# A fused attention and two-layer feed-forward kernel: third tile's loads tied behind the weight loads, VectorE's second conversion pass into a free slot

## Chip, cores and metric

One NeuronCore of a Trainium2 chip runs the whole program in one launch. The metric is the device time of one execution, in microseconds: the median of three runs. TensorE (PE in the profile) multiplies, VectorE (DVE), ScalarE (ACT) and GpSimd (POOL) work elementwise, SyncE (SP) issues most of the transfers.

## What is computed

The weights w_in, w_out (and those of the second layer) come as 64-bit floats, so the kernel converts them itself.

```python
B, H, S, D = 4, 8, 576, 64
# windowed attention: each query sees itself and the 63 keys before it
scores = q @ k.T / sqrt(D); mask = (rel >= 0) & (rel < 64)
attn_out = softmax(scores, mask) @ v            # (4, 8, 576, 64)
x = attn_out.transpose(0, 2, 1, 3).reshape(2304, 512)
# first layer: w_in 512 x 2048, w_out 2048 x 512
h = x @ w_in
g = where(h >= 1, h, where(h <= -1, 0, (h + 1)**2 / 4))
y = g @ w_out
# second layer: w_in 512 x 1024, w_out 1024 x 512, gain g_ln
h = y @ w_in2; s = h * softmax(h)
out = (((s - mean(s)) / sqrt(var(s) + 1e-6)) * g_ln) @ w_out2
```

## The kernel before

Attention works on 12 tiles of 192 tokens, and in each on 4 pairs of heads; g counts these groups (tile t = g // 4). For a group `st_qkt` transposes Q and K into the buffers kq (for the first three tiles on TensorE, L334, with copies by VectorE and ScalarE; from the fourth tile on by VectorE's transposes, L325 and L326), `st_s` makes scores and exponentials, `st_norm` divides, `st_t` transposes the probabilities and `st_v` multiplies by V and leaves x as a high and a low part (xh, xl).

The first layer goes over 6 blocks j of 384 tokens (two tiles) and in each over 16 slices f of 128 columns. `moe_h` makes h of a slice (12 matmuls, L496: high times high, high times low, low times high), `moe_g` and `moe_g2` make g (ScalarE L505, L506 and L512, VectorE's u pass L511), `moe_g3` its low part gl (L516; GpSimd in block 0), `moe_y` adds the slice into four accumulators (L527). Block 0 is special in that the weights arrive while it runs, and in that its two tiles are taken one after the other for the first two slices.

The weights of the first layer are 32 units of 512 KB, two per slice: for slice f the unit of w_in (number 2f + 1) and that of w_out (2f + 2). A unit goes through these steps:

1. load into one of NST = 5 staging buffers `wst` (`w_unit`, L124 and L126, on the SP queue). A staged value is a pair of 32-bit words, low and high;
2. `split_a`: ScalarE rescales the high word (L132);
3. `split_b`: VectorE shifts the low word (L136), then joins the two words (L137). Before, L137 writes its result back over the high word, so with a step of two words;
4. `split_c`: ScalarE casts the result to the high half wih or woh (L145), GpSimd subtracts it for the low half wil or wol (L146). Before, both read the staging buffer, so it is free for the next load when L146 is done.

`w_conv` takes each unit in flight one step on, and is called once per group in the opening and twice per slice after it. Each of the 64 halves has a slot of its own, [128, 512] of 32 bits, in the pool w_p (tags wih0 to wih15, wil, woh, wol); the slots of wih12 to wih15 and wil12 to wil15 hold Q and K of the first two tiles at first. The third tile's Q and K (`qkn`, `load_qk(2 * NP)`) and later ones (`qk`) have five buffers of their own, V (`vw`) has six.

The order on each engine's queue is made by a scheduler: it takes the instructions that the program's text lists, and moves those ahead whose inputs it reckons to be ready. `tc.issue_after(x)` keeps what is issued under it behind the instruction x. `after(fn, a)` uses it for loads: before, x is the first weight load, `wdma[0]`, so that the scheduler was free to put them almost anywhere. On its queue each engine takes its instructions strictly in that order, SP its transfers too.

Of the kernel before, what the change touches and what calls it, by code (L numbers as in the profile page):

```python
# [8 lines left out]
F32 = mybir.dt.float32  # L9
F32R = mybir.dt.float32r  # L10
U32 = mybir.dt.uint32
# [9 lines left out]
def kernel(  # L21
# [12 lines left out]
    nc = tc.nc  # L34
# [83 lines left out]

    wdma = []

    def w_unit(src, hi, lo, gain=None, eng=nc.sync):
        st = stage["p"].tile([128, 512, 2], U32, tag="st", bufs=NST, name="wst")
        if src.shape[0] == 128 and len(src.shape) == 3:
            w_dma = eng.dma_start(out=st.rearrange("p (k f) t -> p k (f t)", k=src.shape[1]), in_=src)  # L124
        else:
            w_dma = eng.dma_start(out=st.rearrange("p f t -> p (f t)"), in_=src)  # L126
        wdma.append(w_dma.ins)
        return st, hi, lo, gain

    def split_a(st, *_):  # L130
        val = st[:, :, 1].bitcast(F32)
        nc.scalar.activation(val, val, ACTF.Prelu, scale=2.0 ** -112, alpha=2.0 ** 32)  # L132

    def split_b(st, *_):
        low, high = st[:, :, 0], st[:, :, 1]
        nc.vector.tensor_scalar(low, low, 29, None, op0=ALU.logical_shift_right)  # L136
        nc.vector.scalar_tensor_tensor(  # L137
            high, high, 3, low, op0=ALU.logical_shift_left, op1=ALU.bitwise_or
        )

    def split_c(st, hi, lo, gain):
        val = st[:, :, 1].bitcast(F32)
        if gain is not None:
            nc.scalar.activation(val, val, ACTF.Copy, scale=gain)
        nc.scalar.copy(hi, val)  # L145
        nc.gpsimd.tensor_tensor(lo, val, as_f32(hi), op=ALU.subtract)  # L146
# [16 lines left out]
        return w_p.tile([128, 512], F32R, tag=tag, name=tag)  # L163

    def w1_unit(f, which):
        if which == 0:
            hi, lo = wtile(f"wih{f}"), wtile(f"wil{f}")
            wih[f] = hi.rearrange("p (k f) -> p k f", k=KC)
            wil[f] = lo.rearrange("p (k f) -> p k f", k=KC)
            src = w_in[:, f * 256:(f + 1) * 256].rearrange("(k p) f -> p k f", p=128)  # L170
        else:
            hi, lo = woh[f], wol[f] = wtile(f"woh{f}"), wtile(f"wol{f}")
            src = w_out[f * 128:(f + 1) * 128, :]
        return w_unit(src, hi, lo)

# [18 lines left out]
    def w2_step(n, act, dve):  # L196
        for age, do in ((0, None), (4, split_a), (5, split_b), (6, split_c)):
# [6 lines left out]
            with tc.issue_after(act), tc.issue_after(dve):  # L204
                if age < 6:
                    do(*w2_units[u])
                    continue
                st, _, _, gain = w2_units.pop(u)
                if u < 8:
                    z = stage["p"].tile([128, 512], F32, tag="st", bufs=NST, name="w2st")  # L210
                    nc.scalar.copy(z, st[:, :, 1].bitcast(F32))
                    nc.gpsimd.dma_start(out=w2d[u], in_=z)
                    continue
                z = stage["p"].tile([128, 2, 512], F32R, tag="st", bufs=NST, name="w2st")
                do(st, z[:, 0, :], z[:, 1, :], gain)
                nc.gpsimd.dma_start(out=w2d[u], in_=as_f32(z.rearrange("p t f -> p (t f)")))

    def w2_load(n):
# [325 lines left out]


    def after(fn, a):
        with tc.issue_after(wdma[0]):
            fn(a)

    def w_load(n=1):  # L550
# [13 lines left out]
    for n in range(G0 + 4):  # L564
# [3 lines left out]
            st_norm(n - 1)  # L568
        if 0 <= n - 2 <= G0:
            st_t(n - 2)  # L570
        if n == NQ:
            after(load_qk, 2 * NP)
        if n == NV:
            after(load_v, 2)
        if n + 2 <= G0 + 1:
            st_qkt(n + 2)
        if 0 <= n - 3 < G0:
# [23 lines left out]
    def slots():  # L601
        for g in range(G0 + 1, GB + 1):
            st_s(g)
            yield
            st_v(g - 1)
            st_norm(g)
            yield
            qkt_and_loads(g + 1)
            v_ahead(g)
            yield  # L610
            st_t(g)
            if g == GB:
                st_s(g + 1)
            yield
# [370 lines left out]
```

## Time and profile before

| what | before |
|---|---|
| three runs, us | 709.12, 710.65, 710.14 (median 710.14) |
| profiled execution, us | 712.67 |
| its span | 710.9 |
| TensorE busy, share of span | 96% |
| VectorE, ScalarE, GpSimd busy | 61%, 58%, 27% |
| DMA moved | 88.94 MB, mean 125 GB/s |
| mean granted TensorE clock (share of full) | 0.993 |

The span runs from the first to the last instruction of the program; the execution has 1.8 us around it. Shares are averages over stages with different limits: the opening with the conversion of the weights (to some 123 us), the rest of the first layer (to some 520 us), the second layer.

### The profile page before, as it was taken

The numbers are of one execution on the slowest core, as the hardware profiler recorded it, in microseconds if no ns is written. First come the engines' busy times: TensorE is split into PE (matmuls) and PEld (weight loads), VectorE is DVE, ScalarE is ACT, GpSimd is POOL, SyncE is SP. The second block draws the span as 40 slices with busy tenths as digits, with TensorE's granted clock in tenths as the row PEclk, the third lists the DMA queues.
The fourth block names the chain that finished last, engine by engine and source line by source line (L and its number), as shares of the span: only waits on it lengthen the run. The fifth ranks groups of instructions, "written<-read, shape, count | busy, mean of one in ns | idle before, by whom it ended". The sixth has DMA issues, their size and how long they took to land.

```text
span 710.9 us, 12663 instructions
## 1 busy us (share of the span) xinstructions
PE 685.6 (96%) x4439; PEld 630.0 (89%) x4439; DVE 434.3 (61%) x1147; ACT 413.0 (58%) x1006; POOL 195.3 (27%) x217
## 2 busy tenths in 40 slices
PE   6899978999999999999999999999999899999998
PEld 5689768999999999999999999999988678888887
DVE  4549898555555555454455543642379799988850
ACT  5778886565566655565566665454455635545541
POOL 2358876200001000021112111652472223300000
PEclk9989999999999999999999999999999999999999
DMA  9986897534353623346352211452033554553321
GB/s 193 216 231 171 220 260 189 107 81 107 71 110 88 139 61 73 78 124 130 87 112 70 95 60 47 154 200 89 1 126 97 175 164 155 175 177 122 131 74 45
DMA packets 155544, 88.94 MB, mean 125 GB/s; under 512 B 118616, under 2 KB 141400, under 8 KB 155480
## 3 DMA queue, kind: packets, MB, share of 16 engines
q1 hardware_dynamic: 144040, 64.00, 36.4%
q0 software_dynamic: 8704, 19.41, 8.4%
q10 hardware_dynamic: 2736, 4.72, 1.8%
q8 instruction: 35, 0.57, 0.4%
q14 instruction: 29, 0.24, 0.1%
HBM read 63.97 MB, written 24.12 MB: 124 GB/s over the span
## 4 chain that ended last, share of the span: by engine, by line
PE 72%; DVE 10%; issue 7%; POOL 4%; DMA 3%; ACT 2%; SPq 1%; DVEq 0%; POOLq 0%; ACTq 0%
PE ps_h L496 22%; PE acc L527 22%; PE ps_o L826 13%; PE P L711 7%; PE ps_x L476 2%; PE ps_p L402 2%; PE ps_s L442 2%; PE ps_s L352 2%; DVE wst L137 2%; POOL wil L249 2%; DVE wst L136 1%; PE ps_x L421 1%; DMA wst<-in_moe_w_out_dram 1%; DVE gl L516 1%; DVE s L740 1%
## 5 line engine op out<-in xcount | busy, mean ns | idle before, releaser
L511 DVE SCALAR_TENSOR_TENSOR u<-u,ps_h 128x384 f32<-128x384 f32 (+1 forms) x98 | 53.2, 543 | 143.8 <-ACT u L506 140.2
L496 PE MATMUL ps_h<-xh,wih 128*128 128x384 f32 (+1 forms) x392 | 132.6, 339 | 3.2 <-DVE u L511 3.1
L496 PE MATMUL ps_h<-xl,wih 128*128 128x384 f32 (+1 forms) x392 | 131.5, 336 | 1.4 <-DVE xl L429 1.4
L527 PE MATMUL acc<-gl,woh 128*128 128x384 f32 (+1 forms) x392 | 130.7, 335 | 2.2 <-DVE gl L516 1.3
L496 PE MATMUL ps_h<-xh,wil 128*128 128x384 f32 (+1 forms) x392 | 131.5, 336 | 0.0
L527 PE MATMUL acc<-gh,wol 128*128 128x384 f32 (+1 forms) x392 | 129.7, 333 | 0.0
L527 PE MATMUL acc<-gh,woh 128*128 128x384 f32 (+1 forms) x392 | 126.9, 342 | 0.0
L505 ACT ACTIVATE u<-ps_h,half 128x384 f32<-128x384 f32 (+1 forms) x98 | 55.9, 572 | 92.6 <-PE ps_h L496 92.4
L512 ACT CAST gh<-u 128x384 fp32r<-128x384 f32 (+1 forms) x98 | 49.7, 507 | 55.0 <-DVE u L511 37.8
L496 PEld LDWEIGHTS ps_h<-xh,wih 128*128 128x128 f32 x392 | 74.6, 190 | 5.2 <-DVE u L511 4.7
L527 PEld LDWEIGHTS acc<-gl,woh 128*128 128x128 f32 x392 | 73.8, 188 | 3.5 <-DVE gl L516 1.7
L496 PEld LDWEIGHTS ps_h<-xl,wih 128*128 128x128 f32 x392 | 74.7, 190 | 2.2 <-DVE xl L429 2.0
L516 DVE TENSOR_TENSOR gl<-u,gh 128x384 fp32r<-128x384 f32 x80 | 52.8, 661 | 37.3 <-ACT gh L512 36.7
L527 PEld LDWEIGHTS acc<-gh,woh 128*128 128x128 f32 x392 | 72.4, 188 | 3.0 <-issue 2.4
L496 PEld LDWEIGHTS ps_h<-xh,wil 128*128 128x128 f32 x392 | 74.7, 190 | 0.1
L527 PEld LDWEIGHTS acc<-gh,wol 128*128 128x128 f32 x392 | 73.7, 188 | 0.0
L711 PE MATMUL P<-wih,x2p 128*128 128x512 f32 x216 | 70.6, 391 | 0.5 <-DVE xo L539 0.5
L826 PE MATMUL ps_o<-woh,wol 128*128 128x512 f32 (+1 forms) x152 | 58.6, 385 | 2.9 <-DVE wol L814 2.9
L826 PE MATMUL ps_o<-woh,woh 128*128 128x512 f32 (+1 forms) x152 | 58.4, 384 | 0.0
L826 PE MATMUL ps_o<-wol,woh 128*128 128x512 f32 (+1 forms) x152 | 58.0, 382 | 0.0
L506 ACT ACTIVATE u<-u 128x384 f32<-128x384 f32 (+1 forms) x98 | 51.0, 521 | 2.0
L711 PEld LDWEIGHTS P<-wih,x2p 128*128 128x128 f32 x216 | 40.5, 188 | 9.2 <-DVE xo L539 0.9
(125 smaller groups left out, 1250.8 us busy)
## 6 DMA issues: line engine op xcount, KB each, us to landing
vw<-in_v_dram SPq DMA_DIRECT2D x32, 256.0 KB, 5.2
wst<-in_moe_w_in_dram SPq DMA_DIRECT2D x16, 512.0 KB, 5.2
wst<-in_moe_w_out_dram SPq DMA_DIRECT2D x16, 512.0 KB, 5.5
lnd<-e SPq DMA_DIRECT2D x16, 512.0 KB, 2.7
lT<-lnd SPq DMA_DIRECT2D x64, 128.0 KB, 3.0
x2d<-xo POOLq DMA_DIRECT2D x24, 192.0 KB, 2.5
out_dram<-o ACTq DMA_DIRECT2D x17, 256.0 KB, 2.9
wst<-in_moe_w_in_dram POOLq DMA_DIRECT2D x8, 512.0 KB, 5.3
```

Source lines behind the costliest of these rows:

```text
L137: nc.vector.scalar_tensor_tensor(high, high, 3, low, op0=ALU.logical_shift_left, op1=ALU.bitwise_or)
L249: nc.gpsimd.tensor_tensor(lo, v_, as_f32(hi), op=ALU.subtract)
L352: nc.tensor.matmul(ps[:, i * 128 + c0:i * 128 + 128], qT[g][:, i, :, :].rearrange("p x q -> p (x q)"), kT[g][:, i * 64 + c0:i * 64 + 128], ...
L496: nc.tensor.matmul(ps, a, bb[:, kc, c], start=(n == 0), stop=(n == 3 * KC - 1))
L505: nc.scalar.activation(u, ps, ACTF.Relu, bias=half, scale=0.5)
L506: nc.scalar.activation(u, u, ACTF.Square)
L511: g = nc.vector.scalar_tensor_tensor(u, u, 1.0, ps, op0=ALU.min, op1=ALU.max)
L512: return nc.scalar.copy(hi, u).ins, g.ins
L516: eng.tensor_tensor(lo, u, as_f32(hi), op=ALU.subtract)
L527: nc.tensor.matmul(acc[j, e][:, c], a, bb, start=(f == 0 and n == 0 and c.start == 0), stop=(f == NF - 1 and n == 2),)
L711: nc.tensor.matmul(ps, l, r, start=(n == 0), stop=(n == 5))
L826: nc.tensor.matmul(ps, a[kk // 4][:, kk % 4, :], b[kk][:, c:c + w], start=(n == 0), stop=(n == 3 * NK2 - 1),)
```

## The change

Two edits. First, `split_b` gets a target `val`: for a w_in unit of slice f that is the slot of woh f, for a w_out unit of slice f the slot of wih f + 3, as long as that exists (f + 3 < 16); both slots are still empty then. The last three w_out units and the units of the second layer keep the high word in the staging buffer as their target. L137 (L139 in the changed kernel) writes there with a step of one word, and `split_c` reads there. Second, `after` ties to the newest weight load instead of the first, the third tile's Q and K are issued three rounds later in the opening (`n == G0 + 3`), and its V when the slots begin.

```diff
-    def w_unit(src, hi, lo, gain=None, eng=nc.sync):
+    def w_unit(src, hi, lo, gain=None, eng=nc.sync, val=None):
...
-        return st, hi, lo, gain
+        if val is None:
+            val = st[:, :, 1].bitcast(F32)
+        return st, val, hi, lo, gain
...
-    def split_b(st, *_):
+    def split_b(st, val, *_):
         low, high = st[:, :, 0], st[:, :, 1]
         nc.vector.tensor_scalar(low, low, 29, None, op0=ALU.logical_shift_right)
         nc.vector.scalar_tensor_tensor(
-            high, high, 3, low, op0=ALU.logical_shift_left, op1=ALU.bitwise_or
+            val.bitcast(U32), high, 3, low, op0=ALU.logical_shift_left, op1=ALU.bitwise_or
         )
 
-    def split_c(st, hi, lo, gain):
-        val = st[:, :, 1].bitcast(F32)
+    def split_c(_, val, hi, lo, gain):
...
     def w1_unit(f, which):
+        tag = f"wih{f + 3}" if which else f"woh{f}"
+        val = w_p.tile([128, 512], F32, tag=tag, name="wv") if f + 3 * which < NF else None
...
-        return w_unit(src, hi, lo)
+        return w_unit(src, hi, lo, val=val)
...
     def after(fn, a):
-        with tc.issue_after(wdma[0]):
+        with tc.issue_after(wdma[-1]):
             fn(a)
...
-        if n == NQ:
+        if n == G0 + 3:
             after(load_qk, 2 * NP)
-        if n == NV:
-            after(load_v, 2)
...
             st_norm(g)
+            if g == G0 + 1:
+                after(load_v, 2)
```

In the rows of order below, a name's number tells one buffer from another. The SP queue in the opening, from the third unit on, before (L279 is Q and K of the third tile, L291 of the fourth, L302 V of the third):

```order
L124 DMA wst_170<-in_moe_w_in_dram 128x4x256
L126 DMA wst_174<-in_moe_w_out_dram 128x1024
L124 DMA wst_178<-in_moe_w_in_dram 128x4x256
L279 DMA qkn_438<-in_q_dram 96x8x64
L279 DMA qkn_439<-in_q_dram 96x8x64
L279 DMA qkn_440<-in_k_dram 128x8x64
L279 DMA qkn_441<-in_k_dram 128x8x64
L291 DMA qk_964<-in_q_dram 32x6x32 x4
L291 DMA qk_964<-in_k_dram 32x6x32 x4
L126 DMA wst_365<-in_moe_w_out_dram 128x1024
L124 DMA wst_413<-in_moe_w_in_dram 128x4x256
L302 DMA vw_474<-in_v_dram 128x8x64
```

And in the changed kernel (three lines further on):

```order
L124 DMA wst_173<-in_moe_w_in_dram 128x4x256
L126 DMA wst_178<-in_moe_w_out_dram 128x1024
L124 DMA wst_183<-in_moe_w_in_dram 128x4x256
L126 DMA wst_371<-in_moe_w_out_dram 128x1024
L124 DMA wst_420<-in_moe_w_in_dram 128x4x256
L126 DMA wst_462<-in_moe_w_out_dram 128x1024
L124 DMA wst_491<-in_moe_w_in_dram 128x4x256
L126 DMA wst_516<-in_moe_w_out_dram 128x1024
L282 DMA qkn_518<-in_q_dram 96x8x64
L282 DMA qkn_519<-in_q_dram 96x8x64
L282 DMA qkn_520<-in_k_dram 128x8x64
L282 DMA qkn_521<-in_k_dram 128x8x64
```

Five units, 6 to 10, have moved ahead of the third tile's Q and K; the fourth tile's loads, not seen here, now come after unit 21.

VectorE between the conversion of the third unit and the second u pass, before (rows of scores and softmax left out at the "..."):

```order
L137 SCALAR_TENSOR_TENSOR wst_170<-wst_170 128x512
L136 TENSOR_SCALAR wst_178<-wst_178 128x512
...
L137 SCALAR_TENSOR_TENSOR wst_174<-wst_174 128x512
L137 SCALAR_TENSOR_TENSOR wst_178<-wst_178 128x512
...
L511 SCALAR_TENSOR_TENSOR u_562<-u_562,ps_h_549 128x192
...
L337 COPY kq0_124<-ps_t_600 64x3x64
L429 TENSOR_TENSOR xl_310<-ps_x_580,xh_309 128x192
L511 SCALAR_TENSOR_TENSOR u_640<-u_640,ps_h_627 128x192
```

And in the changed kernel:

```order
L139 SCALAR_TENSOR_TENSOR wv_170<-wst_173 128x512
...
L139 SCALAR_TENSOR_TENSOR wv_175<-wst_178 128x512
...
L139 SCALAR_TENSOR_TENSOR wv_180<-wst_183 128x512
...
L139 SCALAR_TENSOR_TENSOR wv_368<-wst_371 128x512
L514 SCALAR_TENSOR_TENSOR u_567<-u_567,ps_h_554 128x192
...
L139 SCALAR_TENSOR_TENSOR wv_417<-wst_420 128x512
...
L139 SCALAR_TENSOR_TENSOR wv_459<-wst_462 128x512
...
L139 SCALAR_TENSOR_TENSOR wv_488<-wst_491 128x512
L139 SCALAR_TENSOR_TENSOR wv_513<-wst_516 128x512
L514 SCALAR_TENSOR_TENSOR u_653<-u_653,ps_h_640 128x192
```

The second conversion passes of units 6 to 10 now stand ahead of the second u pass, and the copy of the third tile's Q (kq0) behind it.

ScalarE around that copy, in the changed kernel (L146 is the cast to the high half, L134 `split_a`, L410 a copy of transposed probabilities, L509 the square and L515 the cast of g, L341 and L342 the copies of Q and K of the third tile's first group):

```order
L146 CAST wih3_418<-wv_417 128x512
L146 CAST woh2_369<-wv_368 128x512
L134 ACTIVATE wst_516<-wst_516 128x512
L509 ACTIVATE u_653<-u_653 128x192
L146 CAST wih4_489<-wv_488 128x512
L410 COPY pT_620<-ps_p_619 128x384
L146 CAST woh3_460<-wv_459 128x512
L515 CAST gh_654<-u_653 128x192
L146 CAST woh4_514<-wv_513 128x512
L341 COPY kq0_124<-ps_t_611 64x3x64
L342 COPY kq0_124<-ps_t_611 128x256
```

Before, no cast of units 6 to 10 stood ahead of these copies. The cast to woh f writes the slot that has held the values of w_in unit f, and so waits for GpSimd's subtraction for wil f; in woh2, woh3 and woh4 that is the subtraction for wil2, wil3 and wil4. Here the cast to wih3 has been put ahead of that to woh2, and the cast to wih4 ahead of that to woh3.

## Rows read from the trace of the kernel before

**Rows 1.** page, part 1: busy us (share of the span) and instructions of each engine

```profile
PE 685.6 (96%) x4439; PEld 630.0 (89%) x4439; DVE 434.3 (61%) x1147; ACT 413.0 (58%) x1006; POOL 195.3 (27%) x217
```

**Rows 2.** windows: busy us (and instructions) of each engine, granted clock, DMA share, GB/s

```profile
14.00:53.00 39.00, 35.05 (x273) 30.57 (x274) 20.50 (x90) 30.00 (x102) 17.97 (x21) 0.91 0.99 221
...
53.00:123.00 70.00, 62.84 (x416) 57.44 (x415) 66.21 (x132) 55.49 (x136) 54.56 (x42) 1.00 0.83 214
...
140.00:690.00 550.00, 545.31 (x3501) 504.31 (x3500) 332.18 (x857) 306.82 (x706) 114.26 (x137) 1.00 0.39 109
```

**Rows 3.** line groups of TensorE, 80 to 110 us: shapes, count | busy us, mean ns | idle us before

```profile
L496 PE MATMUL ps_h<-xh,wih 128*128 128x384 f32 x16 | 5.8, 364 | 2.7 <-DVE u L511 2.7
```

**Rows 4.** line groups of TensorE, 180 to 210 us

```profile
L496 PE MATMUL ps_h<-xh,wih 128*128 128x384 f32 x26 | 8.7, 334 | 0.0
```

**Rows 5.** line groups of VectorE, 53 to 123 us

```profile
L137 DVE SCALAR_TENSOR_TENSOR wst<-wst 128x512 uint32<-128x512 uint32 x25 | 28.9, 1165 | 0.6 <-ACT wst L132 0.4
...
L136 DVE TENSOR_SCALAR wst<-wst 128x512 uint32<-128x512 uint32 x24 | 19.4, 809 | 2.4 <-DMA wst<-in_moe_w_out_dram 2.4
```

**Rows 6.** line groups of VectorE, 14 to 53 us

```profile
L137 DVE SCALAR_TENSOR_TENSOR wst<-wst 128x512 uint32<-128x512 uint32 x7 | 5.5, 781 | 1.9 <-ACT wst L132 1.8
...
L136 DVE TENSOR_SCALAR wst<-wst 128x512 uint32<-128x512 uint32 x8 | 3.3, 415 | 0.0
```

**Rows 7.** timeline of VectorE, from 56 us: start us, us, instruction, count

```profile
57.24 3.52 DVE L137 SCALAR_TENSOR_TENSOR wst<-wst 128x512 uint32<-128x512 uint32 x2
```

**Rows 8.** timeline of GpSimd, the same stretch

```profile
57.00 1.50 POOL L146 TENSOR_TENSOR wol<-wst,woh 128x512 fp32r<-128x512 f32 x1
...
58.46 1.75 POOL L146 TENSOR_TENSOR wil<-wst,wih 128x512 fp32r<-128x512 f32 x1
```

**Rows 9.** timeline of the SP queue, from 17 us

```profile
20.98 1.47 SPq L279 DMA_DIRECT2D qkn<-in_q_dram  x2
...
22.50 6.08 SPq L279 DMA_DIRECT2D qkn<-in_k_dram  x2
...
33.41 0.36 SPq L126 DMA_DIRECT2D wst<-in_moe_w_out_dram  x1
```

**Rows 10.** instructions of line L146, second layer: min/median/max ns, first and last start

```profile
L146 POOL TENSOR_TENSOR w2st<-wst,w2st x8: 1293/1304/1311, 315.1 to 440.7; 128x512 fp32r<-128x512 f32 x8
```

**Rows 11.** instructions of line L249, a subtraction with dense inputs

```profile
L249 POOL TENSOR_TENSOR wil<-w2t,wih x8: 1295/1301/1628, 466.3 to 500.1; 128x512 fp32r<-128x512 f32 x8
```

**Rows 12.** line groups of ScalarE, 53 to 123 us

```profile
L132 ACT ACTIVATE wst<-wst 128x512 f32<-128x512 f32 x24 | 16.3, 680 | 1.0 <-DMA wst<-in_moe_w_in_dram 0.7
...
L145 ACT CAST woh<-wst 128x512 fp32r<-128x512 f32 x13 | 8.8, 674 | 7.0 <-DVE wst L137 6.8
```

**Rows 13.** instructions of line L248, a cast with a dense input

```profile
L248 ACT CAST wih<-w2t x8: 614/616/616, 465.4 to 499.4; 128x512 fp32r<-128x512 f32 x8
```

**Rows 14.** timeline of VectorE, from 32 us

```profile
32.09 1.05 DVE L137 SCALAR_TENSOR_TENSOR wst<-wst 128x512 uint32<-128x512 uint32 x1
...
34.85 0.80 DVE L137 SCALAR_TENSOR_TENSOR wst<-wst 128x512 uint32<-128x512 uint32 x1 [0.44 <-ACT wst L132]
```

**Rows 15.** timeline of ScalarE, from 70 and from 100 us

```profile
74.33 0.66 ACT L145 CAST woh<-wst 128x512 fp32r<-128x512 f32 x1
...
101.77 0.67 ACT L145 CAST woh<-wst 128x512 fp32r<-128x512 f32 x1 [0.80 <-DVE wst L137]
```

**Rows 16.** timeline of GpSimd, from 71 and from 100 us

```profile
75.13 1.50 POOL L146 TENSOR_TENSOR wil<-wst,wih 128x512 fp32r<-128x512 f32 x1
...
101.14 1.77 POOL L146 TENSOR_TENSOR wil<-wst,wih 128x512 fp32r<-128x512 f32 x1
```

**Rows 17.** timeline of TensorE, from 40 us: first transposes of the third tile

```profile
42.27 0.55 PE L334 MATMUL ps_t<-ident,qkn 96*128 96x96 f32 x4
```

**Rows 18.** instructions of the staging buffers, up to 160 us: min/median/max ns, first, last start

```profile
L137 DVE SCALAR_TENSOR_TENSOR wst<-wst x32: 649/766/1806, 14.9 to 121.1; 128x512 uint32<-128x512 uint32 x32
```

**Rows 19.** line groups of GpSimd, 53 to 123 us

```profile
L516 POOL TENSOR_TENSOR gl<-u,gh 128x384 fp32r<-128x384 f32 x11 | 13.3, 1212 | 3.1 <-ACT gh L512 3.0
```

More of the change, by code (lines that the diff above doesn't have):

```diff
@@ L207, in w2_step @@
                     continue
-                st, _, _, gain = w2_units.pop(u)
+                st, val, _, _, gain = w2_units.pop(u)
                 if u < 8:
                     z = stage["p"].tile([128, 512], F32, tag="st", bufs=NST, name="w2st")
-                    nc.scalar.copy(z, st[:, :, 1].bitcast(F32))
+                    nc.scalar.copy(z, val)
                     nc.gpsimd.dma_start(out=w2d[u], in_=z)
@@ L214, in w2_step @@
                 z = stage["p"].tile([128, 2, 512], F32R, tag="st", bufs=NST, name="w2st")
-                do(st, z[:, 0, :], z[:, 1, :], gain)
+                do(st, val, z[:, 0, :], z[:, 1, :], gain)
                 nc.gpsimd.dma_start(out=w2d[u], in_=as_f32(z.rearrange("p t f -> p (t f)")))
```

## Prediction

> **What bounds the kernel now.** The page first: TensorE is busy in 96% of the span [rows 1]. The reader should take from it that nothing off TensorE can pay except where TensorE is short of work. The windows show where that is: from 140 to 690 us it is busy in 545 of 550 us; from 53 to 123 us in 62.8 of 70 [rows 2]. Busy is not full, either: 80 to 110 us holds 16 matmuls of one form of the first product, 180 to 210 us, the same length, holds 26 [rows 3, 4]; the granted clock is 1.00 in the windows around both [rows 2]. Each group is one of three alike there, so about a third of the large matmuls that 30 us can take are missing, some 10 us in that stretch alone. That is the room which a change of the front can use; as TensorE is nearly always busy from 140 us on, time won in the front should stay won to the end.
>
> What holds TensorE back there is the conversion of the weights, 32 units of 512 KB. From 53 to 123 us VectorE is busy in 66.2 of 70 us, ScalarE in 55.5, GpSimd in 54.6 [rows 2]. VectorE's two conversion passes alone (L136 and L137) are 19.4 and 28.9 us of it [rows 5]. Part of that is waiting: L137 takes a mean of 1165 ns there and L136 809, against 781 and 415 from 14 to 53 us [rows 5, 6]. The timelines show why: two L137 fill 57.24 to 60.76 us, 1.76 each, while GpSimd runs subtractions from 57.00 and from 58.46 us [rows 7, 8]. From 14 to 53 us, on the other hand, VectorE is busy in 20.5 of 39 us: 18.5 us are idle, since the units are not there. The SP queue issues the third tile's Q and K at 20.98 and 22.50 us and the sixth unit only at 33.41 [rows 9].
>
> **The change, part by part.**
>
> *Dense target of L137.* 29 of 32 units get it (16 of w_in, 13 of w_out). It removes no instruction. No row has L137 with a dense target. Nearest rows: GpSimd's subtraction takes 1304 ns on strided values and 1301 on dense ones [rows 10, 11]; ScalarE's cast takes 674 strided and 616 dense [rows 12, 13]. So for L137 I bound it by 0 and 0.06 us each way, at most 1.7 us over 29, and take 0, as GpSimd's subtraction, also with two inputs, shows. ScalarE wins 29 x 0.06 = 1.7 us, beside other work: 0.
>
> *The staging buffer.* Before, a buffer was free after GpSimd's subtraction, the last of the four steps; now it is after L137, a cast (0.67) and a subtraction (1.3 to 1.8) earlier. A load then waits for VectorE in place of GpSimd.
>
> *Third tile's loads.* Q and K go behind unit 10, V behind unit 11; the next tiles' small loads, tied to the newest unit, also go later. With both edits, SP can issue units 6 and 7 at about 21 us, units 8 to 10 after L137 of units 3 to 5 (the first ends at 33.1, the last at 35.7 us [rows 14]). VectorE's order confirms it: ahead of the second u pass stood 5 L137, now 10.
>
> *The gain.* Five units move from the full stretch into idle time. There they took 0.81 + 1.17 = 1.97 us of VectorE each: 5 x 1.97 = **9.9 us** off the stretch that VectorE fills. In the early stretch they cost 5 x (0.415 + 0.781) = 6.0 us, under 18.5 idle: 0 for VectorE. ScalarE is tighter: 5 x (0.68 + 0.67) = 6.8 us [rows 12] into 39 - 30.0 = 9.0 idle [rows 2]. Behind it stand softmax exponentials and Q and K copies that TensorE waits for. Bounds 0 and 6.8; nearer to 0, as the idle time holds it, yet not in the right places: I take a quarter, **1.5 us** lost.
>
> *The new waits.* The free slot in which a w_in unit's values now stand is the slot of the high half of the next w_out unit. So ScalarE's cast into that slot must wait for GpSimd's subtraction of the w_in unit. Where the order puts the next w_in unit's cast ahead, the wait is covered; for seven casts past 53 us it does not. In the trace of before most of the seven begin after that subtraction has ended; two do not: one cast starts at 74.33 us and the subtraction ends at 75.13 + 1.50 = 76.63, 2.3 us; the other at 101.77 against 101.14 + 1.77 = 102.91, 1.1 us [rows 15, 16]. Bounds 0 and 7 x 2.3 = 16; I take the trace's own **3.4 us**. Queued behind the cast on ScalarE are Relu, Square and the cast gh of the large product, for which VectorE's u pass and then TensorE wait. The 14.5 us that ScalarE is idle in this stretch [rows 2] can hide some of it.
>
> *Sum:* -9.9 + 1.5 + 3.4 = **-5.0 us**. The profiled execution took 712.67 us (span 710.9, 1.8 around it); the sum makes it 707.7. It lies 2.5 above the median of the runs, 710.14; the same 5.0 off the median gives **705.1 us**. A measurement of this kernel can tell about 0.2%, 1.4 us, from no change.
>
> *A rule against it.* GpSimd's subtractions and VectorE's L136 and L137 stretch each other [rows 5 to 8]. The Trainium skill (SBUF — State Buffer, "SBUF: two separate sides") says that the two engines share a port pair as an exclusive lock, held for a whole instruction, by a VectorE instruction with two SBUF inputs or in a two-port mode. The trace agrees with a lock: 1.76 us each against 0.65 undisturbed. What it would make of the time is the third rival.
>
> **The rivals.**
>
> *1. ScalarE behind GpSimd.* The new wait takes back the gain: at 0.75 us for each of the thirteen casts of the full stretch [rows 12] it is 9.8 against 9.9, and the time is 710. For it: the order has two such casts close together just ahead of the third tile's Q and K copies. Against it: GpSimd is idle 15.4 of 70 us [rows 2]. At 0.6 us for each the time is 708.
>
> *2. The third tile comes too late (the slower side).* TensorE takes its transposes in order; in before the first starts at 42.27 us [rows 17]. Now Q and K (0.9 MB) stand behind units 8 to 10 (1.5 MB), which cannot start before 33.1 us. At the 221 GB/s of 14 to 53 us [rows 2], 2.4 MB take 10.9 us: the last lands at 44.0, the first of the four some 3 us sooner. TensorE's order has eight more matmuls ahead of the first transpose, at most 0.36 us each [rows 3] and less where they overlap, so it asks between 42.3 and 45.2: just in time. Every us by which VectorE's passes or the queue slip is a us for which TensorE stands, with the whole first block behind it, and the granted clock, 0.91 over this stretch [rows 2], could sink further. To pass the gain by 1.4 us, TensorE must lose 6.4: last landing past 50 us, the queue at 140 GB/s. With 7.5 us lost the time is 712.6. It decides from 50 us on; a loss of 2 or 3 us leaves it faster.
>
> *3. The pair of engines is full anyway.* If GpSimd's and VectorE's conversion work excluded each other strictly, the full stretch would be set by their sum. Subtraction 1.30 [rows 10], L137 0.65 undisturbed [rows 18] and L136 0.42 [rows 6]: 2.4 us for each unit, 24 to 25 units 58 us, and the gl subtractions 13.3 more [rows 19], the softmax products not counted: 71 in a stretch of 70. That is full, or a little more than strict exclusion allows. Yet taking five units out takes 12 us out of that sum too. It gives no gain only if the early stretch were full as well, and GpSimd is busy for 18.0 of 39 us there [rows 2]. Time 710.
>
> *4. The scheduler's lead is not kept.* In the order of after, VectorE has 10 L137 against 5 ahead of the second u pass, but only 23 against 21 ahead of the tenth. If VectorE were ahead by those two alone when the block's end is set, the gain is 2 x 1.97 = 3.9 less the 4.9 of losses: 711 at worst, 706 without the losses. By the last passes the lead is all 32 in both, so what counts is idle time filled, which is why the forecast keeps five.
>
> **How the numbers follow.** The forecast (gain of 2 to 9 us) gets 0.60. A gain beyond it, when ScalarE's losses hide in its idle time (9.9 whole: 700.2), 0.05. Rivals 1 and 4 together 0.17, near 709, of which 0.07 counts as faster by over 0.2%, 0.07 as no change, 0.03 as slower. Rival 2 gets 0.13, rival 3 0.05 (no change). Faster 0.72, same 0.12, slower 0.16. The range runs from 700.0, the gain without losses, to 712.0, short of rival 2's 712.6; about 0.13 lies outside. The likeliest case's own range is 701 to 708.
>
> **What would show it.** In the profile after: the last L137 of the 32 units starting some 5 to 10 us before the 121.1 us of now [rows 18]; the sixth and seventh unit issued near 21 us; L137 still near 0.65 us undisturbed; TensorE's shortage in 80 to 110 us smaller; from 140 us on nothing but a shift. Idle time of ScalarE ahead of woh casts, ended by GpSimd's subtraction, would show rival 1, and TensorE waiting for Q and K near 43 us rival 2. The prediction is wrong if the units are converted five ahead at 50 us and the last one still ends at 120.

## The result, and the profile after

| what | before | after |
|---|---|---|
| median of the runs taken together, us | 709.63 (708.94 to 710.65) | 717.48 (716.04 to 717.84) |
| profiled execution, its span, us | 712.67, 710.9 | 717.82, 716.0 |
| mean granted TensorE clock | 0.993 | 0.985 |

The ratio is 1.0106, with a 95% interval of 1.0085 to 1.0126: slower by 7.8 us, where 705.1 and at most 712.0 was forecast.

The page's first part of the kernel after has TensorE at the same share as [rows 1]:

```profile
PE 688.7 (96%) x4439; PEld 634.2 (89%) x4439; DVE 432.7 (60%) x1147; ACT 412.0 (58%) x1006; POOL 193.3 (27%) x217
```

The windows of [rows 2] (columns as there):

```profile
14.00:53.00 39.00, 32.24 (x234) 27.57 (x235) 25.29 (x79) 28.87 (x92) 21.81 (x22) 0.91 0.95 228
53.00:123.00 70.00, 61.81 (x403) 57.42 (x403) 56.07 (x137) 53.40 (x141) 47.12 (x38) 0.91 0.79 206
140.00:690.00 550.00, 546.04 (x3523) 506.30 (x3522) 332.54 (x865) 308.02 (x714) 114.81 (x138) 1.00 0.40 111
```

This is the surprise of the case. VectorE got its relief: from 53 to 123 us it is busy in 56.1 us instead of 66.2, 10.1 less, where five units of 1.97 us are 9.9. The make-up is another: the stretch holds three fewer passes of each kind than [rows 5], 22 of L139 and 21 of L138, not five, and they are shorter (L138 695 ns against 809). TensorE gained nothing: 61.8 instead of 62.8, at a granted clock of 0.91 instead of 1.00. The finer windows show two holes, at 40 to 60 and at 100 to 120 us. After:

```profile
40.00:50.00 10.00, 7.46 (x54) 6.65 (x53) 7.29 (x14) 5.93 (x16) 7.38 (x7) 0.83 1.17 228
50.00:60.00 10.00, 7.97 (x45) 6.81 (x45) 5.57 (x19) 7.70 (x23) 6.73 (x6) 0.66 1.10 311
60.00:100.00 40.00, 38.43 (x275) 36.46 (x275) 33.41 (x80) 32.58 (x84) 29.27 (x24) 1.00 0.70 187
100.00:120.00 20.00, 14.34 (x89) 12.96 (x87) 15.54 (x35) 12.40 (x34) 11.95 (x11) 0.83 0.91 229
```

The same windows of the kernel before:

```profile
40.00:50.00 10.00, 9.48 (x91) 8.79 (x90) 5.25 (x19) 7.21 (x24) 4.68 (x5) 0.92 0.71 202
50.00:60.00 10.00, 9.74 (x80) 9.45 (x81) 8.40 (x20) 9.73 (x27) 5.76 (x6) 1.00 0.62 161
60.00:100.00 40.00, 35.27 (x229) 31.66 (x229) 37.38 (x76) 32.59 (x76) 32.48 (x25) 1.00 0.87 226
100.00:120.00 20.00, 17.94 (x120) 16.25 (x118) 19.10 (x42) 14.63 (x40) 14.59 (x13) 1.00 0.98 245
```

Busy time hides much of it, since a matmul at the lower clock level counts double. A better measure is the columns of all matmuls that start in a stretch, added up over the trace's rows; in the steady part TensorE does 66.3 thousand in 30 us (180 to 210 us of the kernel before), 2.2 thousand a us. From 40 to 60 us it did 30.0 thousand before and 13.8 after, 7.3 us of work less; from 60 to 100 us 65.9 and 74.5, 3.9 us more; from 100 to 120 us 34.4 and 22.4, 5.5 us less. By 140 us 15.4 thousand are missing, 7.0 us, and up to 560 us it stays at 14 to 17 thousand. The two spans differ by 5.1 us only: the profiled execution of the kernel before, itself 3.0 us over the median, does 5.1 thousand columns fewer than the other from 560 to 580 us.

In 40 to 60 us the windows show two losses, not one: TensorE is idle for 4.6 us instead of 0.8, and the granted clock is at its lower level for 10.2 us instead of 1.6 (a clock of 0.83 over 10 us is 3.4 us at half the full clock).

**The first hole.** The SP queue did what was forecast: units 6 and 7 at 20.4 and 20.9 us, 8 to 10 from 33.3, then Q and K (timeline):

```profile
20.41 0.43 SPq L126 DMA_DIRECT2D wst<-in_moe_w_out_dram  x1
20.93 0.39 SPq L124 DMA_DIRECT2D wst<-in_moe_w_in_dram  x1
33.30 0.34 SPq L126 DMA_DIRECT2D wst<-in_moe_w_out_dram  x1
...
37.22 0.34 SPq L126 DMA_DIRECT2D wst<-in_moe_w_out_dram  x1
37.61 1.00 SPq L282 DMA_DIRECT2D qkn<-in_q_dram  x2
38.66 3.38 SPq L282 DMA_DIRECT2D qkn<-in_k_dram  x2
```

The last of Q and K landed at 46.60 us. What TensorE then waited for was not the transfer but the copies behind it: ScalarE had two casts of units 8 and 10 ahead of them, each waiting for GpSimd. The copy that VectorE makes (48.85 us) was not held by conversions: VectorE had been idle for 2.54 us ahead of it. The timelines of ScalarE, GpSimd and TensorE (in brackets the idle time before an instruction and what ended it):

```profile
49.67 0.62 ACT L146 CAST woh<-wv 128x512 fp32r<-128x512 f32 x1 [1.60 <-POOL wil L147]
50.32 0.31 ACT L341 COPY kq<-ps_t 64x192 f32<-64x192 f32 x1
50.64 0.37 ACT L342 COPY kq<-ps_t 128x256 f32<-128x256 f32 x1
```

```profile
48.37 1.27 POOL L147 TENSOR_TENSOR wil<-wv,wih 128x512 fp32r<-128x512 f32 x1
```

```profile
43.91 0.27 PE L530 MATMUL acc<-gl,woh 128*128 128x192 f32 x1
44.02 0.27 PE L530 MATMUL acc<-gh,wol 128*128 128x192 f32 x1
...
47.33 0.41 PE L499 MATMUL ps_h<-xl,wih 128*128 128x192 f32 x1
47.54 0.41 PE L499 MATMUL ps_h<-xh,wil 128*128 128x192 f32 x1
...
51.07 0.94 PE L355 MATMUL ps_s<-kq 128*128 128x128 f32 x6 [1.63 <-ACT kq L342]
```

Matmuls of 192 columns start 0.11 us apart at 44 us and 0.21 at 47.5 us: the lower clock level. VectorE's conversions held TensorE before that. The part xl (L432) could be made from 41.06 us on, when ScalarE has its input xh done; VectorE is then in a second pass and has a first pass to do ahead of xl, and TensorE waits 1.25 us. VectorE, ScalarE and TensorE:

```profile
39.54 1.52 DVE L138 TENSOR_SCALAR wst<-wst 128x512 uint32<-128x512 uint32 x1
40.99 1.09 DVE L139 SCALAR_TENSOR_TENSOR wv<-wst 128x512 uint32<-128x512 uint32 x1
42.00 0.42 DVE L138 TENSOR_SCALAR wst<-wst 128x512 uint32<-128x512 uint32 x1
42.33 0.34 DVE L432 TENSOR_TENSOR xl<-ps_x,xh 128x192 fp32r<-128x192 f32 x1
```

```profile
40.76 0.30 ACT L431 CAST xh<-ps_x 128x192 fp32r<-128x192 f32 x1
```

```profile
42.73 0.36 PE L499 MATMUL ps_h<-xl,wih 128*128 128x192 f32 x1 [1.25 <-DVE xl L432]
```

Nor are the early passes the short ones of [rows 6]. Line groups of VectorE, 14 to 53 us:

```profile
L139 DVE SCALAR_TENSOR_TENSOR wv<-wst 128x512 uint32<-128x512 uint32 x11 | 11.2, 1021 | 2.3 <-ACT wst L134 2.3
L138 DVE TENSOR_SCALAR wst<-wst 128x512 uint32<-128x512 uint32 x11 | 6.7, 609 | 0.0
```

The window of 50 to 60 us has 0.66, which is 6.8 of its 10 us at the lower level; before, it had none.

**The second hole** is one VectorE operation of 64 columns. It took 1.06 us in the kernel before (at 106.40) and 3.84 here, while GpSimd ran three operations end to end, and TensorE stood 4.34 us. VectorE, GpSimd and TensorE after:

```profile
108.81 3.84 DVE L385 TENSOR_TENSOR p<-p,rs 128x64 f32<-128x64 f32 x1
112.57 0.41 DVE L389 TENSOR_TENSOR p<-p,rs 128x256 f32<-128x256 f32 x1
```

```profile
109.09 1.30 POOL L147 TENSOR_TENSOR wol<-wst,woh 128x512 fp32r<-128x512 f32 x1
110.35 1.26 POOL L147 TENSOR_TENSOR wil<-wv,wih 128x512 fp32r<-128x512 f32 x1
111.57 0.99 POOL L519 TENSOR_TENSOR gl<-u,gh 128x384 fp32r<-128x384 f32 x1
```

```profile
112.79 0.39 PE L403 MATMUL ps_p<-ident,p 128*64 128x128 f32 x1 [4.34 <-DVE p L385]
```

A VectorE operation that lasts over two or more of GpSimd's is not new. The kernel before has one of 2.60 us at 112.84, and in all eight of the twenty traces of this case have one of 2.6 to 4.0 us between 108 and 122 us. In the kernel before it is a conversion pass, and TensorE has no wait of over 0.8 us there; here it is an operation that TensorE waits for. Timelines of VectorE, before and then in e6 (an experiment of the next section):

```profile
112.84 2.60 DVE L136 TENSOR_SCALAR wst<-wst 128x512 uint32<-128x512 uint32 x1
```

```profile
112.28 4.00 DVE L380 TENSOR_SCALAR sm<-sm 128x3 f32<-128x3 f32 x1
```

Of the other rows: L139 on dense targets is as fast undisturbed as L137 was in [rows 18], and its last pass starts at 122.7 us, not earlier than the 121.1 of there; the large products of 80 to 110 us are 20, against the 16 of [rows 3]. Instructions of the staging buffers, and the TensorE group:

```profile
L139 DVE SCALAR_TENSOR_TENSOR wv<-wst x29: 649/687/1760, 14.8 to 119.3; 128x512 uint32<-128x512 uint32 x29
L139 DVE SCALAR_TENSOR_TENSOR wst<-wst x3: 693/695/1315, 103.7 to 122.7; 128x512 uint32<-128x512 uint32 x3
```

```profile
L499 PE MATMUL ps_h<-xh,wih 128*128 128x384 f32 x20 | 7.1, 356 | 0.8 <-DVE u L514 0.8
```

### The profile page after: what moved, and what is told of

It is laid out like the page before. It is cut to its first block, busy times and chain, and to the rows that moved or that the text cites. A ratio compares the mean times of both kernels' runs of the same rounds, so it can differ in the third digit from the quotient of the medians.

```text
span 716.0 us, 12633 instructions
## 1 busy us (share of the span) xinstructions
PE 688.7 (96%) x4439; PEld 634.2 (89%) x4439; DVE 432.7 (60%) x1147; ACT 412.0 (58%) x1006; POOL 193.3 (27%) x217
## 4 chain that ended last, share of the span: by engine, by line
PE 79%; DVE 8%; ACT 4%; DMA 3%; POOL 2%; issue 2%; SPq 0%; DVEq 0%; POOLq 0%; ACTq 0%
PE ps_h L499 25%; PE acc L530 25%; PE ps_o L829 12%; PE P L714 7%; PE ps_x L479 2%; PE ps_p L405 2%; PE ps_s L445 2%; PE ps_s L355 2%; DVE wv L139 1%; DVE gl L519 1%; ACT p L369 1%; PE ps_x L424 1%; DVE wst L138 1%; DMA qk<-in_q_dram 1%; DMA x2r<-x2d 1%
## 5 line engine op out<-in xcount | busy, mean ns | idle before, releaser
L515 ACT CAST gh<-u 128x384 fp32r<-128x384 f32 (+1 forms) x98 | 49.6, 506 | 61.9 <-DVE u L514 44.7
L509 ACT ACTIVATE u<-u 128x384 f32<-128x384 f32 (+1 forms) x98 | 51.1, 522 | 2.0
```

The costliest lines, as they stand in the source:

```text
L509: nc.scalar.activation(u, u, ACTF.Square)
L515: return nc.scalar.copy(hi, u).ins, g.ins
```

## The experiments

In the table, thousands of columns are of the program's own matmuls (added ones left out), from the profiled execution; the clock is the granted clock of 50 to 60 us. The ratio is of all executions, the columns are of one: that of e4 took 712.07 us (median 713.92), that of e15 713.67 (716.52), that of e6 721.07 (717.74). Columns and ratio of a row need not agree in the small.

| kernel | ratio to before (95%) | columns 40–60 | 60–100 | 100–120 | by 140 | clock |
|---|---|---|---|---|---|---|
| before | 1 | 30.0 | 65.9 | 34.4 | 186.5 | 1.00 |
| after | 1.0106 (1.0085–1.0126) | 13.8 | 74.5 | 22.4 | 171.1 | 0.66 |
| e1_slot_alone | 1.0002 (0.9986–1.0018) | 29.5 | 62.8 | 36.7 | 188.4 | 1.00 |
| e2_loads_alone | 1.0077 (1.0047–1.0106) | 14.3 | 73.2 | 33.9 | 178.4 | 0.84 |
| e4_other_slot | 1.0055 (1.0032–1.0077) | 22.1 | 72.4 | 34.0 | 189.3 | 1.00 |
| e6_ahead2 | 1.0102 (1.0060–1.0144) | 14.7 | 69.5 | 28.2 | 171.1 | 0.66 |
| e8_behind7 | 1.0052 (1.0029–1.0074) | 20.4 | 70.8 | 32.0 | 183.4 | 0.66 |
| e9_other_slot_behind7 | 1.0054 (1.0028–1.0080) | 16.3 | 73.4 | 30.7 | 180.6 | 0.66 |
| e13_qk_late | 1.0156 (1.0115–1.0197) | 14.5 | 53.1 | 38.8 | 164.6 | 0.50 |
| e14_v_late | 1.0089 (1.0055–1.0122) | 19.0 | 70.1 | 33.9 | 182.3 | 0.52 |
| e15_held | 1.0076 (1.0054–1.0097) | 27.1 | 60.0 | 34.9 | 181.1 | 1.00 |
| e18_filler | 1.0017 (1.0002–1.0032) | 16.3 | 71.8 | 32.4 | 180.0 | 0.83 |
| e22_small | 1.0035 (1.0016–1.0054) | 13.5 | 71.3 | 31.6 | 175.4 | 0.66 |
| e26_norm_act | 1.0059 (1.0037–1.0082) | 13.2 | 74.1 | 35.8 | 176.5 | 0.66 |

**One half of the change alone.** e1 has the slot, with the loads as before; e2 has the loads, and L139 writes in place:

```diff
-        val = w_p.tile([128, 512], F32, tag=tag, name="wv") if f + 3 * which < NF else None
+        val = w_p.tile([128, 512], F32, tag=tag, name="wv") if False else None
```

> The free slot alone, all loads tied and placed as before. Theory A (ScalarE's casts to woh wait for GpSimd's subtraction just ahead of the third tile's Q and K copies): the casts still wait, but no longer in that place, since the third tile comes early: 709 to 712 us. Theory B (the third tile's loads come too late for TensorE's order, whatever the slot): 708 to 711, as before. Theory C (the small Q and K loads of later groups stand in a block ahead of unit 23 on the SP queue and take the lead of the units away): 708 to 711. If the slot by itself is a loss, 713 or more.

> The later loads alone; the second conversion pass writes into the staging buffer as before, so no cast waits for a subtraction. Theory A: without that wait the loss is gone, 709 to 713 us. Theory B: the loss stays, 716 to 719. Theory C: the loss stays, since 32 small loads stand in a row on the SP queue, 715 to 718.

The slot alone changes nothing, the late loads alone give 0.77 of the 1.06%. The loss comes with the loads. In e2 the last of Q and K landed at 50.42 us, later than in the changed kernel, so e2 does not tell the transfer from the conversions.

**The casts that wait for GpSimd.** e4 puts a w_in unit's values into a slot two slices on, so that no cast overwrites what GpSimd still reads:

```diff
-        tag = f"wih{f + 3}" if which else f"woh{f}"
-        val = w_p.tile([128, 512], F32, tag=tag, name="wv") if f + 3 * which < NF else None
+        tag = f"wih{f + 3}" if which else f"woh{f + 2}"
+        val = w_p.tile([128, 512], F32, tag=tag, name="wv") if f + 2 + which < NF else None
```

> The change, but a w_in unit's values go to the slot of the w_out unit two slices on instead of the same slice's, so that ScalarE's next cast waits for no subtraction; the loads stay late. Theory A: 710 to 713 us, and the wait of some 1.6 us ahead of the third tile's copies is gone. Theory B: 716 to 718. Theory C: 716 to 718, as 32 small loads stand in a row ahead of a unit.

1.0055: half of the loss. The 40 to 60 us stretch gets back 8.3 of 16.2 thousand columns, and keeps its clock. The casts' waits for GpSimd are gone, and TensorE's wait for the copies is 0.74 us instead of 1.63, in the place that the first rival had named. But TensorE's idle time in this stretch is not smaller, 5.3 us against 4.6, as it waits elsewhere (1.79 us for gl, 1.14 for xl and as much for the probabilities). What came back in this trace came with the clock. The windows of e4:

```profile
40.00:50.00 10.00, 6.76 (x65) 5.77 (x61) 7.48 (x20) 6.92 (x18) 7.99 (x7) 1.00 1.15 229
50.00:60.00 10.00, 7.98 (x66) 7.50 (x67) 5.95 (x19) 8.27 (x28) 5.98 (x8) 1.00 1.14 291
```

**The block of small loads on SP.** After unit 22 (72.68 us) the changed kernel's SP queue issues 24 loads of later Q and K before unit 23 (86.21). e6 issues those two groups ahead instead of four.

```diff
-        if m >= NPE and m + 4 < NG:
-            load_qk(m + 4)
+        if m >= NPE and m + 2 < NG:
+            load_qk(m + 2)
...
-            for z in range(1, 5):
+            for z in range(1, 3):
```

> The change, with the small Q and K loads from the fourth tile on issued two groups ahead instead of four, which spreads them among the weight units on the SP queue; everything up to the eighth u pass stands as in the change. Theory A and theory B: the loss of 40 to 60 us stays, 716 to 718. Theory C: unit 23 is issued near 75 us instead of 86.2, the second shortage of TensorE at 100 to 120 us goes, and the time is 711 to 714 us.

The lead was kept: unit 23 went out at 78.08 us, and the last second pass started at 109.5, 13 us sooner than in the changed kernel. Timeline of SP and instructions of e6:

```profile
78.08 0.39 SPq L124 DMA_DIRECT2D wst<-in_moe_w_in_dram  x1
```

```profile
L139 DVE SCALAR_TENSOR_TENSOR wst<-wst x3: 658/680/1779, 99.8 to 109.5; 128x512 uint32<-128x512 uint32 x3
```

It earned nothing (1.0102). So the conversions' last unit does not set the end of the front. This speaks against the basis of the forecast, though the first hole is there in e6 as well.

**Which loads, and how late.** e13 puts V back, e14 Q and K; e8 lets Q and K go behind unit 7; e9 is e8 with the slot of e4. In e13 and e14 the later tiles' loads stay tied as in the change. The edit of e8:

```diff
-        if n == G0 + 3:
+        if n == NQ:
             after(load_qk, 2 * NP)
```

> The changed kernel with the third tile's V loads back at their former place; its Q and K stay behind unit 10. VectorE has six and seven units done at the first two u passes and ten at the third tile's first copy. Theory B (late Q and K cost): 714 to 719 us, as the changed kernel. Theory D (early conversions cost, by how many stand ahead of the second u pass): seven in place of ten, so about half of the loss, 712 to 715 us. If V alone is what comes too late: 709 to 712 us.

> The changed kernel with the third tile's Q and K loads back at their former place; its V alone stays late. VectorE has five and six units done at the first two u passes and five and eight at the third tile's first copies. Theory B (late Q and K cost) and theory D (early conversions cost): both 708 to 712 us, as before. If V alone is what comes too late: 715 to 719 us.

> The changed kernel with the third tile's Q and K behind unit 7 instead of unit 10; V late as in the change. VectorE has six and seven units done at the first two u passes and seven and ten at the third tile's first copies. Theory B (each unit ahead of Q and K delays them): SP can issue unit 7 near 21 us and then Q and K at once, about 15 us sooner than in the changed kernel, so 709 to 712 us. Theory D: seven ahead of the second u pass, one or two more than before, 710 to 714 us. Faster than the kernel before (under 708) only if the lead of the conversions pays for itself.

> The third tile's Q and K behind unit 7 and the dense target of a w_in unit in a slot that nothing reads or subtracts at that time, so that no cast of ScalarE waits for GpSimd's subtraction of the unit before. Each of the two alone took about half of the loss away (1.0106 to 1.0052 and 1.0055). If they are two separate costs: 708 to 711 us. If both act on the same waits of 40 to 60 us: 712 to 715 us, as each alone.

Late V costs 0.9% with Q and K early (717.7 us, the third case of its expectation, against both theories); Q and K late with V early is the worst of all; behind unit 7 instead of 10 halves the loss. e8 and e4 do not add up: both together give 1.0054, as the expectation has it if they act on the same waits. That they do is not shown: e9 has 16.3 thousand columns in 40 to 60 us, fewer than either alone. In each of these kernels conversions are ahead of the third tile's copies, and each has too few columns in 40 to 60 us.

**The conversions held back.** In e15 the loads are as late as in the change, but VectorE's passes from the sixth unit on are tied behind the u passes (HOLD is 4), and three early calls of `w_conv` are left out:

```diff
-            split_b(*w_b[-1])
+            if pin is None:
+                split_b(*w_b[-1])
+            else:
+                with tc.issue_after(pin):
+                    split_b(*w_b[-1])
...
-            w_conv()
+            if n > 1:
+                w_conv(pin=pins[1] if n <= HOLD else None)
```

> The changed kernel with one thing held back: from the sixth unit on, VectorE's two conversion passes are tied behind the u passes, so that VectorE has five units done at the first two u passes (six and ten in the changed kernel) and seven at the third tile's first two copies (ten and eleven). The loads and the dense targets are those of the changed kernel, the third tile is as late. Theory B (the third tile's Q and K come too late, whatever VectorE does): nothing comes back, 715 to 719 us, and TensorE's shortage from 40 to 60 us stays. Theory D (the loss is the early conversions themselves, which stand ahead of the softmax's small operations, the second u pass and the third tile's copies in VectorE's fixed order): the shortage of 40 to 60 us goes, 708 to 712 us.

The windows of e15:

```profile
50.00:60.00 10.00, 8.82 (x70) 8.21 (x69) 8.46 (x24) 8.22 (x26) 4.26 (x5) 1.00 1.04 229
60.00:70.00 10.00, 8.49 (x66) 7.81 (x65) 7.62 (x18) 7.36 (x19) 10.00 (x7) 1.00 0.84 283
70.00:80.00 10.00, 7.42 (x31) 7.00 (x30) 9.97 (x15) 8.72 (x20) 8.09 (x7) 0.72 0.52 131
```

This is the cleanest result on the first hole. With the third tile nearly as late as in the change (last landing at 45.57 us instead of 46.60), 40 to 60 us has 27.1 thousand columns and a clock of 0.99 and 1.00 in its two windows: the hole comes with the conversions that stand ahead of the attention's operations, not with the transfer. But the time is only 1.0076: GpSimd is full from 60 to 70 us, and TensorE stands 2.58 us for gl at 74.96. The work that was held back meets the next stretch. Theory D was right on the place and wrong on the time (716.5 us, where it had 708 to 712).

**The clock behind the waits.** e18 adds 36 matmuls whose results are overwritten, where TensorE waits, to the changed kernel; e19 to the kernel before, e20 to e8. e22 and e23 have them with 16 columns instead of 192, e24 has 60 of them in the kernel before, e25 36 with the slot alone.

```diff
+    def warm(ps, n):
+        for _ in range(n):
+            nc.tensor.matmul(ps[:, 0:192], wih[0][:, 0, :], xh[0][:, 0, 0:192], start=True, stop=True)
...
         ps = at_bank("ps_s")
+        warm(ps, {8: 8, 9: 8, 10: 8}.get(g, 0))
```

> The changed kernel with 36 idle-time matmuls of 192 columns, on operands that are long there, into banks that the matmuls behind them overwrite: four ahead of the ps_p transposes of groups 7 to 9, eight ahead of the ps_s matmuls of groups 8 to 10, where TensorE waits between 44 and 62 us. Nothing else that is computed changes. Theory K (what the waits of 40 to 60 us cost is doubled by the granted clock, which falls to its lower level from about 46 to 61 us behind them): the granted clock of 50 to 60 us is near 1.00 instead of 0.66, and the time falls to 711 to 714 us. Theory D alone (the waits cost by themselves, the clock adds nothing): 717 to 719 us, as the changed kernel or up to 2 us more for the added matmuls.

> The control: the kernel before with the same 36 matmuls, where the granted clock of 50 to 60 us is at its full level already. Both theories: 710 to 714 us, as before plus at most 36 x 0.11 = 4 us. If the fillers made a kernel faster by something other than the clock, it would show here as a time below 709.

> The third tile's Q and K behind unit 7, with the same 36 matmuls. That kernel without them had a granted clock of 0.66 in 50 to 60 us. Theory K: near 1.00 there, 709 to 712 us, and under 708 if the lead of the conversions then pays. Theory D alone: 714 to 717 us.

> The changed kernel with the 36 added matmuls at the same places of the order, each of 16 columns instead of 192: the order of instructions without the activity. Theory K (the granted clock): the clock of 50 to 60 us is again near 0.66 and the time 715 to 718 us, as the changed kernel. Theory O (the new order of the other instructions did it): 711 to 713 us, as with 192 columns.

> The kernel before with the 36 added matmuls of 16 columns. With 192 columns its ratio was 0.998 (0.9964 to 0.9995). Theory K: 0.999 to 1.002, as before. Theory O: 0.996 to 0.999.

> The kernel before with 60 added matmuls of 192 columns, eight ahead of ps_s of groups 7 to 11 and four ahead of ps_p of groups 7 to 10, so that the clock is held from 38 us on. Theory K: the lower level of 40 to 50 us (0.92 in the kernel before) goes, 0.996 to 1.000; the later added matmuls stand where TensorE is mostly busy and cost up to 24 x 0.11 = 2.6 us, so 1.000 to 1.003 if they are not hidden. Theory O makes no forecast.

> The slot edit alone (loads as before) with the 36 added matmuls of 192 columns. Theory K: the slot alone had the clock at 1.00 in 40 to 60 us already, so 0.997 to 1.001, as the kernel before with the same matmuls. If the slot's earlier units earn something once the clock is kept: 0.995 or less.

e18 looked like proof of theory K: 1.0017, and the clock of 50 to 60 us up to 0.83. The control e22 took most of it away: 1.0035 with 16 columns and a clock of 0.66 again. The windows of 50 to 60 us, e18 and then e22:

```profile
50.00:60.00 10.00, 8.14 (x61) 7.63 (x62) 4.17 (x19) 7.22 (x23) 6.15 (x6) 0.83 1.07 302
```

```profile
50.00:60.00 10.00, 7.42 (x49) 6.91 (x50) 3.38 (x13) 5.90 (x19) 6.26 (x6) 0.66 1.13 320
```

So some 0.7% came with the new order of instructions that the added matmuls brought. What is left between e22 and e18 is 0.18%, with overlapping intervals, and their orders are the same only up to 87 us. Nor is the pair a test of a full clock: by the clocks of the two windows of 40 to 60 us, the lower level lasts 10.2 us in the changed kernel, 7.4 in e22 (0.97, 0.66) and 5.4 in e18 (0.90, 0.83). The 2.0 us between the last two are worth some 1.0 us of work at half the clock, 0.14% (an estimate). What a full clock would give back stays open.

In the kernel before the pair has the same order throughout, and it reads alike: 0.9980 (0.9964 to 0.9995) with 192 columns, 0.9997 (0.9978 to 1.0016) with 16. e20 gave 0.9992 (0.9976 to 1.0007) with a clock of 1.00 in 50 to 60 us, as theory K forecast; it has no control with 16 columns. e24, 1.0078 (1.0061 to 1.0094), and e25, 1.0053 (1.0034 to 1.0071), went against K's forecasts, each with its own new order; their added columns, 10.8 and 6.9 thousand, are 4.9 and 3.1 us at the steady rate, where nothing hides them. e19 is the only kernel whose interval lies below 1, and only just.

**The second hole alone.** e26 moves one normalisation from VectorE to ScalarE; every engine's order is the same up to it. e27 is the same edit in the kernel before.

```diff
+    ACTN = (13,)
...
+        if u in ACTN:
+            for i in range(QB):
+                c0 = 64 if first(t, i) else 0
+                nc.scalar.activation(p[:, i, c0:], p[:, i, c0:], ACTF.Copy, scale=rs[:, i:i + 1])
+            return
         eng = nc.gpsimd if t < 3 else nc.vector
```

> The changed kernel with one softmax normalisation moved: the second group of the fourth tile is multiplied by ScalarE in three activations instead of by VectorE in two, so that it cannot wait for GpSimd's two subtractions and its gl pass, which ran end to end from 109.09 to 112.56 us while VectorE's 128x64 operation took 3.84 us. All instructions stand in the same order up to there. Theory E (that wait is a cost of its own: 4.3 us of TensorE's time, and the lower granted clock of 110 to 120 us behind it): 710 to 714 us. If the time lost there only moves on to the next wait (the loss is what the stretch of 40 to 62 us lost, wherever it shows): 716 to 719 us.

> The control: the same edit in the kernel before, where the same operation took 1.06 us (106.40 us). Theory E: 0.998 to 1.001, as before or a microsecond less. If the edit or the order that it changes behind that place earned or cost something by itself, it shows here.

The windows of e26:

```profile
100.00:110.00 10.00, 8.55 (x55) 7.49 (x55) 7.90 (x20) 8.22 (x23) 7.20 (x6) 1.00 0.92 217
110.00:120.00 10.00, 10.00 (x69) 9.50 (x69) 8.67 (x19) 8.21 (x23) 7.09 (x7) 1.00 0.84 236
```

The hole is gone (35.8 thousand columns against 22.4), and with it 0.0047 of the ratio, some 3.3 us; the control is 0.9991 (0.9972 to 1.0010). The time, 715.9 us, lies between the two cases of the expectation, and the second, that the lost time only moves on, holds for a part: 120 to 140 us loses 8.0 thousand of the 13.4 won (31.4 against 39.4). What is left, 1.0059, is near e2 and e15.

## Why the prediction was wrong

- **Price of the dense target, 0:** right. 0.649 us at least in both, ScalarE's dense casts 0.62.
- **When the units can be loaded:** right within 1.5 us (20.4, 20.9, and 33.3 to 37.2 us).
- **"They cost 5 x (0.415 + 0.781) = 6.0 us, under 18.5 idle: 0 for VectorE":** this is the step that failed. VectorE did have the idle time, and used it (25.3 us busy in 14 to 53 us instead of 20.5). Two things were wrong. The price: the early passes are no longer the short ones of before. Eleven of each take 17.9 us, where seven and eight took 8.8 [rows 6]: 9.1 us more, for three or four units and not five. GpSimd now works beside them: the first pass of 39.54 us takes 1.52 us beside its subtractions, that of 42.00, with GpSimd idle, 0.42. And the path: VectorE's order is fixed, and the passes stood ahead of small operations of the attention, of xl (TensorE waits 1.25 us) and of the second u pass, and their casts and subtractions ahead of the third tile's copies. TensorE lost 16.2 thousand columns, 7.3 us, instead of the 1.5 taken for ScalarE; with 3.8 us more of idle time and 8.6 more at the lower clock, each is about half of it (an estimate). e15 shows the path: same loads, conversions behind, 27.1 thousand columns instead of 13.8.
- **"-9.9 us off the stretch that VectorE fills":** VectorE lost 10.1 us of work there and TensorE gained 3.9 us, in 60 to 100 us only. So a part of the gain came, 3.9 us. But the last unit was not the limit of the front: e6 had all units converted 13 us sooner and gained nothing. A busy share of 95% had been read as a bound; that the chain from softmax to product and back is the bound instead fits the waits, and no run here tests it alone.
- **New waits, 3.4 us:** that casts would wait for subtractions was right, the place was wrong. The prediction priced seven casts past 53 us; what hurt were two at 47.2 and 49.7 us (0.33 and 1.60 us idle), just ahead of the third tile's copies. Without them, in e4, half of the loss is gone, in its trace by way of the clock. The first rival had named the place but asked for 9.8 us in the full stretch.
- **The second rival,** the slower side, was the nearest: its 7.5 us lost are the size of the first hole (7.3). But its condition, a last landing past 50 us, was not met (46.60); it took the transfer for the wait, where the queues of ScalarE and VectorE were. It had named VectorE's passes and a lower clock as what could make it worse, and both did. With its chance of 0.13 and a gain of 9.9 set against it, its time came to 712.6 and the range ended below the result.
- **The third rival's lock** cost time in another way than by the sum of the two engines' work: by one operation that TensorE waits for, 3.84 us at 108.81, 0.47% of the time by e26. Which operation is caught is luck of the order; the kernel before had a conversion pass there.
- **The sentence that would prove it wrong** came true: ten units' second passes were done at 46.04 us, and the last one of all still started at 122.7.

How much of the first hole is each of lateness, conversions and clock, in time and not in columns, stays open: each kernel that mends it has another order behind it, and a new order nearly alone moved the time by some 0.7% (e22 against the changed kernel).

## What to carry to other kernels

Idle time of an engine is free only at the places of its order where nothing that the bottleneck waits for stands behind; before moving work into it, read which small operations follow, and what ends TensorE's next wait. A full engine is a bound only if the bottleneck's waits end at it: take its work away in one experiment before building on it. And when a probe changes a scheduler's order, run the same order without the effect (here 16 columns for 192); the first reading of e18, 0.9% for the clock, shrank to 0.2% for what the added matmuls did.

## What the hardware showed that was not expected

- In the changed kernel the granted clock was at its lower level for 3.4 of the ten us from 40 on and for 6.8 of those from 50 on, with TensorE busy in 7.5 and 8.0 of them; at 110 to 120 us again for 6.8, where TensorE had stood 4.34 us up to 112.79. Idle time alone does not tell when: in 40 to 60 us e4 had 5.3 us of it, more than the 4.6 here, and a clock of 1.00.
- A VectorE operation of 64 columns can last over several GpSimd operations: 3.84 us at 108.81, against 0.22 at 98.9. The Trainium skill (SBUF — State Buffer, "SBUF: two separate sides") has the port pair go to whichever of the two starts first, for one instruction, while the other blocks. The trace agrees with the blocking, not with the turn: by the profile VectorE's operation began 0.28 us ahead of the first of three GpSimd operations and ended after the third. GpSimd's DMA issue of 108.34 us, 0.73 long, lay over that start and may have held the pair here. It is not needed for a long hold: in e6 an operation of three columns began while GpSimd subtracted, with no DMA issue beside it, and ended at 116.28 us, after the next three GpSimd operations (112.74 to 116.26, end to end).
